# Token mixing of a gated MLP: the seventh feature chunk as seven block products on 64-column tiles of the matmul array

## Chip, cores, metric

One core of a Trainium2 chip. The metric is the device time of one execution in microseconds (us); medians are given with the lowest and highest run. Within 2% of the kernel before counts as "same".

Engines are named as in the profile: PE is TensorE's matmul, PEld its weight loads, DVE is VectorE, ACT is ScalarE, POOL is GpSimd, SP is SyncE, which here issues nearly all transfers. "Mixing" is the stage that multiplies by `w_sp`.

## The reference, cut to what matters

```python
x = A_x                                        # 1 x 2048 x 512, bf16
h = x + _A_ref(_layernorm(x), A_wqkv, A_wo)    # linear attention: num / den, times wo
h2 = h + _B_ref(_layernorm(h), B_w_in, B_w_sp, B_b_sp, B_w_out)

def _B_ref(x, w_in, w_sp, b_sp, w_out):        # w_in 512 x 1792, w_sp 2048 x 2048, w_out 896 x 512
    z = _gelu(x @ w_in)
    z1, z2 = z[..., :896], _layernorm(z[..., 896:])
    g = einsum('ts,bsf->btf', w_sp, z2) + b_sp[None, :, None]   # the token mixing
    return (z1 * g) @ w_out
```

The 896 features are seven chunks of 128.

## The kernel before: the parts that the change and the argument touch

Every operation is recorded with what it reads and writes. `ORDER` is a packed list that fixes the order of all operations on all engines, transfers included; it was searched in advance.

Six of the seven chunks are mixed in pairs (k, k + 3) by `cell`, with seven block products in place of eight (Strassen-Winograd). The combined operands t1, t2, t4 (of `w_sp`) and s1, s2, s4 (of z2) are made on VectorE. The seventh chunk is a plain product, twice 16 matmuls in each of two passes over pairs of token groups.

```python
def matmuls(out_ap, pairs, start=True, stop=True, onto=False, **k): ...   # one matmul for each (a, b) of pairs

def cell(k, lo, hi):                      # two chunks, two token groups: seven products of 8 matmuls
    ...
    matmuls(bank(A), [(z2[:, s, fl], wsp[:, s, lo]) for s in ss])
    act(bank(B), bank(A), ACT.Copy, GW)
    matmuls(bank(E), [(s1[:, s, :], t1[:, s, :]) for s in ss])
    ...

for p in range(NG // 2):
    lo, hi = (slice(tg * GW, (tg + 1) * GW) for tg in (p, p + NG // 2))
    last = KF - 1
    for tok, b in ((lo, EB[0]), (hi, EB[1])):           # the seventh chunk, plain
        matmuls(bank(b), [(z2[:, s, last * P:KF * P], wsp[:, s, tok]) for s in range(NT)])
        gate(last, tok, b, bsp[:, tok])
    ... combine(t1 ...), combine(t2 ...), combine(t4 ...)
    for k in range(HF):
        ... combine(s1 ...), combine(s2 ...), combine(s4 ...)
        cell(k, lo, hi)
```

Three further places play a part in what follows: the warm-up of PE at the start, the denominators of the attention, and the last sums with their stores.

```python
warmup(34, 103)                                          # 34 matmuls of 128 columns; 16 more a little later

for tg in range(NG):                                     # denominators of a token group
    PE(... zc x pqT on four tiles of 32 columns ...)
    act_exp(r_t, ..., ACT.Ln); act_exp(rcp, r_t, ACT.Exp, scale=-1.0)
    for c in range(KD): spread(first, c, ...)            # SP: four transfers r<-rcp, spread over the partitions
    dve(... tensor_tensor(pqT, pqT, r, ALU.mult) ...)    # needs those transfers
for n in range(NT):
    matmuls(bank(b), [(pqT[:, c, ...], m[:, c, :]) ...]) # "m,pqT" in the profile: needs that multiply

... tensor_tensor(h, psum, h) ...; store(n, slice(0, D), h[:, n, :])   # SP issues most of the stores
```

## Time and profile before

| | before |
|---|---|
| time, median (range) | 230.46 us (230.15 to 230.71, 3 runs) |
| span of the profiled execution | 228.4 us |
| from the start to the sum over pk | 44.48 us |
| from there to the first product with `win` | 19.68 us |
| from there to the last product with `win` | 43.05 us |
| mixing and output: from there to the start of the last matmul | 118.29 us |
| tail: from there to the end | 2.86 us |

The five stages are read from the start times of PE's groups in the timeline; they add up to the span. PE is the bound in all of them.

### The profile page before, as it was taken

The page shows a single profiled execution, that of the slowest core. Times are in us where ns is not written, and L with a number is a line of the kernel's source. Part 1 is how long each engine was busy: PE and PEld are TensorE (multiplying, and loading weights), DVE is VectorE, ACT ScalarE, POOL GpSimd, SP SyncE. Part 2 cuts the span into 40 slices and gives each one's busy share as a digit, 9 for nine tenths or more (in the row PEclk, how much of TensorE's full clock was granted, in tenths as well). Part 3 has the DMA queues.
Part 4 walks back from the last instruction along what each step waited for, and adds up shares of the span by engine and source line. Part 5 has one row for each costly group of instructions (what it writes and reads, how often), then busy time and mean ns, then how long its engine had stood idle before and what let it go on. Part 6 is the DMA issues. An engine that isn't in the chain of part 4 may idle for free.

```text
span 228.4 us, 3248 instructions
## 1 busy us (share of the span) xinstructions
PE 221.9 (97%) x1168; PEld 110.1 (48%) x1191; DVE 174.5 (76%) x349; ACT 108.5 (48%) x203; POOL 47.1 (21%) x134
## 2 busy tenths in 40 slices
PE   7999999999999999999999999999999999999995
PEld 7444444453344444544444444444455556555453
DVE  3899656638999786679998869864988985574395
ACT  5695753389989988999762010300021311122010
POOL 4444300000562694138820000000000000000000
PEclk9999999999999999999999999999999999999999
DMA  6736449927566244599904999200000002010004
GB/s 192 240 77 139 93 110 377 252 70 182 115 126 129 46 95 92 115 210 187 182 1 90 196 192 203 58 0 0 3 0 0 24 26 92 0 46 3 0 23 161
DMA packets 58896, 23.68 MB, mean 104 GB/s; under 512 B 48512, under 2 KB 58752, under 8 KB 58880
## 3 DMA queue, kind: packets, MB, share of 16 engines
q1 hardware_dynamic: 58176, 22.88, 44.2%
q10 hardware_dynamic: 704, 0.59, 0.9%
q8 instruction: 9, 0.15, 0.3%
q14 instruction: 7, 0.06, 0.1%
HBM read 7.47 MB, written 2.10 MB: 42 GB/s over the span
## 4 chain that ended last, share of the span: by engine, by line
PE 87%; DMA 4%; DVE 3%; ACT 3%; issue 1%; POOL 1%; SPq 1%; DVEq 0%
PE psum L402 69%; PE psum L659 6%; PE psum L813 6%; PE psum L816 4%; DMA x<-in_A_x_dram 2%; DMA hnT<-hn 1%; DVE st L510 1%; ACT ct L421 1%; SPq L432 1%; ACT pqT L421 0%; PE psum L724 0%; PE psum L680 0%; ACT z L421 0%; DVE h L988 0%; ACT sh L421 0%
## 5 line engine op out<-in xcount | busy, mean ns | idle before, releaser
L421 ACT ACTIVATE psum<-psum 128x256 f32<-128x256 f32 (+1 forms) x39 | 17.7, 468 | 86.7 <-PE psum L402 55.5
L402 PE MATMUL psum<-wsp,z 128*128 128x512 bf16 x201 | 47.8, 379 | 0.4
L402 PEld LDWEIGHTS psum<-wsp,z 128*128 128x128 bf16 x208 | 20.3, 98 | 23.0
L421 ACT ACTIVATE e<-psum 128x1024 bf16<-128x1024 f32 (+1 forms) x18 | 16.7, 927 | 14.1 <-PE psum L402 13.1
L402 PE MATMUL psum<-t,s 128*128 128x512 bf16 x95 | 22.3, 379 | 0.1
L402 PE MATMUL psum<-wsp 128*128 128x256 bf16 (+1 forms) x87 | 18.9, 313 | 0.2
L421 ACT ACTIVATE z1T<-psum 128x512 bf16<-128x512 f32 x28 | 15.7, 600 | 6.3 <-PE psum L402 5.7
L996 DVE TENSOR_TENSOR u<-psum,bsp 128x512 bf16<-128x512 f32 x16 | 11.0, 688 | 9.4 <-PE psum L402 9.2
L813 PE MATMUL psum<-win,hnT 128*128 128x512 bf16 x63 | 16.4, 379 | 0.3 <-DMA hnT<-hn 0.3
L402 PE MATMUL psum<-wout,z1T 128*128 128x256 bf16 (+1 forms) x81 | 16.2, 313 | 0.0
L659 PE MATMUL psum<-pk,xn 128*128 128x512 bf16 x64 | 15.3, 379 | 0.0
L402 PE MATMUL psum<-xnT,wqkv 128*128 128x512 bf16 x61 | 15.1, 379 | 0.2
L402 PE MATMUL psum<-m,pqT 128*128 128x512 bf16 x62 | 14.6, 380 | 0.4 <-DVE h L787 0.2
L402 PE MATMUL psum<-wqkv,xnT 128*128 128x512 bf16 x61 | 14.7, 379 | 0.2
L421 ACT ACTIVATE z<-psum 128x896 bf16<-128x896 f32 x16 | 14.4, 919 | 0.8 <-PE psum L816 0.5
L402 PEld LDWEIGHTS psum<-t,s 128*128 128x128 bf16 x96 | 9.4, 98 | 10.0
L581 DVE TENSOR_SCALAR e<-e 128x1024 bf16<-128x1024 bf16 (+1 forms) x18 | 7.0, 391 | 8.1 <-ACT e L421 7.9
L816 PE MATMUL psum<-win,hnT 128*128 128x384 bf16 x64 | 13.0, 326 | 0.0
L510 DVE BATCH_NORM_STATS2 st<-x 128x6 f32<-128x512 bf16 x15 | 9.9, 674 | 3.8 <-DMA x<-in_A_x_dram 3.8
L996 DVE TENSOR_TENSOR u<-psum,p 128x512 bf16<-128x512 f32 x12 | 8.3, 688 | 5.8 <-PE psum L402 5.8
L787 DVE SCALAR_TENSOR_TENSOR h<-psum,x 128x512 bf16<-128x512 f32 x16 | 10.7, 686 | 1.8 <-PE psum L402 1.7
L402 PEld LDWEIGHTS psum<-wsp 128*128 128x128 bf16 x90 | 8.7, 98 | 6.8 <-DVE wsp L1001 0.4
(126 smaller groups left out, 378.3 us busy)
## 6 DMA issues: line engine op xcount, KB each, us to landing
r<-rcp SPq DMA_DIRECT2D x16, 128.0 KB, 2.6
out_dram<-h SPq DMA_DIRECT2D x15, 128.0 KB, 1.7
win<-in_B_w_in_dram SPq DMA_DIRECT2D x2, 896.0 KB, 7.2
x<-in_A_x_dram SPq DMA_DIRECT2D x6, 256.0 KB, 4.3
wqkv<-in_A_wqkv_dram SPq DMA_DIRECT2D x2, 512.0 KB, 5.7
wout<-in_B_w_out_dram SPq DMA_DIRECT2D x1, 896.0 KB, 7.2
wo<-in_A_wo_dram SPq DMA_DIRECT2D x1, 512.0 KB, 5.9
bsp<-in_B_b_sp_dram SPq DMA_DIRECT2D x1, 512.0 KB, 4.4
```

The lines of the kernel that those rows point to most:

```text
L402: inst = pe.matmul(out_ap, lhsT=a, rhs=b, start=start and i == 0, stop=stop and i == len(pairs) - 1, **kw)
L421: return g.add("ACT", lambda ac: ac.activation(out_ap, in_ap, func, **kw), [in_ap, *extra], [out_ap] + ([accum] if accum is not None else []),
L432: return g.add(eng, lambda q: q.dma_start(out_ap, in_ap), [in_ap], [out_ap], cost=issue, lat=lat, dma=name, **k)
L510: dve(lambda v: v.bn_stats(s[:, 0:6], src[:, n, :]), [src[:, n, :]], [s[:, 0:6]], D)
L581: dve(lambda v: v.tensor_scalar(e, e, 1.0, EPS_PHI, op0=ALU.min, op1=ALU.add), [e], [e], w * GW, acc=4)
L659: inst = pe.matmul(bank(CB[c]), lhsT=xn[:, i, c * P:(c + 1) * P], rhs=pk[:, i, :], start=i == 0, stop=i == NT - 1)
L787: dve(lambda v, n=n, b=b, s=s: v.scalar_tensor_tensor(h[:, n, :], bank(b), 1.0, x[:, n, :], op0=ALU.mult, op1=ALU.add, accum_out=s[:, 0:1] ...
L813: pe.matmul(bank(b), lhsT=hnT[:, c, n * P:(n + 1) * P], rhs=win2[:, c, 0:GW], start=c == 0, stop=c == KD - 1)
L816: inst = pe.matmul(bank(b + 1, F2), lhsT=hnT[:, c, n * P:(n + 1) * P], rhs=win2[:, c, GW:FH], start=c == 0, stop=c == KD - 1)
L996: dve(lambda v: v.tensor_tensor(t, bank(b), add, ALU.add), [bank(b), add], [t], GW, ps=True)
```

## The change

The intent: seven block products for eight also for the seventh chunk. Split in halves of 64 features, its products have only 64 weight columns, half the array's width. So two of them run side by side on two column tiles, between the products of the other chunks. The arithmetic saves an eighth of 64 matmul steps.

```diff
-ORDER = "c-jTQ17HvU00h8Cwq47%ZQHhO...          (cut: the order of all operations, searched anew)
+ORDER = "c-jrs19Bh;00q&HBxBpQZQHhO...
+    def halves(pairs):                          # two products, matmul by matmul in turn
+        ...
+            for s in range(max(len(a) for _, a, _ in pairs)):
+                for o, a, start in pairs:
+                    if s < len(a):
+                        inst = pe.matmul(o, lhsT=a[s][0], rhs=a[s][1], start=start and s == 0, ...)
+    def last_cell(lo, hi):
+        ...
+        halves([(pb(Y, L), [(z2[:, s, fl], wsp[:, s, lo]) for s in ss], True),
+                (pb(Y, U), [(z2[:, HT + s, fh], t4[:, s, :]) for s in ss], True)])
+        act(pb(X, U), pb(Y, L), ACT.Copy, GW)
+        halves([...])                           # one product in two half sums, 4 pairs
+        halves([(pb(E, L), [(s1[:, s, :], t1[:, s, :]) for s in ss], True),
+                (pb(X, U), [(s2[:, s, :], t2[:, s, :]) for s in ss], False)])
+        act(pb(X, L), pb(X, U), ACT.Copy, GW)
+        halves([...])
+        ... four sums out of PSUM on VectorE, two gates
     for p in range(NG // 2):
-        last = KF - 1
-        for tok, b in ((lo, EB[0]), (hi, EB[1])):
-            matmuls(bank(b), [(z2[:, s, last * P:KF * P], wsp[:, s, tok]) for s in range(NT)])
-            gate(last, tok, b, bsp[:, tok])
...
         for k in range(HF):
+            if k == C6[p]:
+                ... four combinations of z2's blocks in the first pass
+                last_cell(lo, hi)
```

## The prediction

> **What bounds the kernel now.** I read the engine totals first, then the chain of work that ended last, then the stretches of the mixing stage, and last the TensorE timeline around the only place where the kernel already uses column tiles.
>
> ```profile
> span 228.4 us, 3248 instructions
> ...
> PE 221.9 (97%) x1168; PEld 110.1 (48%) x1191; DVE 174.5 (76%) x349; ACT 108.5 (48%) x203; POOL 47.1 (21%) x134
> ...
> PE 87%; DMA 4%; DVE 3%; ACT 3%; issue 1%; POOL 1%; SPq 1%; DVEq 0%
> ```
>
> TensorE is busy for 97% of the span and carries 87% of the chain. A busy PE need not be a dense one, so I compared counts with time in three stretches (end of the gated MLP's input products; first half of the token mixing; second half with the output products). The columns are the stretch, its length, then busy time and count of PE, PEld, DVE, ACT, POOL, then clock and DMA.
>
> ```profile
> 66.00:107.50 41.50, 41.29 (x204) 19.98 (x207) 33.20 (x79) 38.38 (x79) 22.18 (x59) 1.00 0.61 122
> 107.50:161.00 53.50, 53.24 (x246) 24.07 (x249) 43.23 (x71) 14.15 (x26) 7.21 (x17) 1.00 0.55 103
> 161.00:223.00 62.00, 61.68 (x344) 34.13 (x350) 46.26 (x93) 10.40 (x26) 0.00 (x0) 1.00 0.06 20
> ```
>
> In 107.5 to 161 us there are nearly only matmuls of 512 columns: 53.5 us over 246 records is 0.217 us each, at a granted clock of 1.00. Neighbouring matmuls of one product start 0.216 us apart, so PE starts one whenever the array can take it. The few steps of twice that length come about once in 50 matmuls, always 431 or 432 ns: lost records, not waits. From 66 us to the end PE never waits for anything by more than some tens of ns. So what the change is worth is what it takes from, or adds to, PE's own stream. VectorE has 53.5 - 43.2 = 10.3 us idle in the first stretch of mixing and 62.0 - 46.3 = 15.7 us in the second.
>
> Now the cost of a column tile. The sum over pk is sixteen matmuls, four side by side on tiles of 32 columns, between two normal products (start, length, what, count):
>
> ```profile
> 43.52 1.03 PE L659 MATMUL psum<-pk,xn 128*128 128x512 bf16 x4
> 44.48 1.05 PE L680 MATMUL psum<-pk,ones 128*32 128x512 bf16 x16
> 45.46 1.04 PE L659 MATMUL psum<-pk,xn 128*128 128x512 bf16 x4
> ...
> 44.48 0.55 PEld L680 LDWEIGHTS psum<-pk,ones 128*32 128x32 bf16 x16 [0.42 <-issue]
> 45.46 0.55 PEld L659 LDWEIGHTS psum<-pk,xn 128*128 128x128 bf16 x4 [0.42 <-issue]
> ```
>
> Two things are to be seen. Sixteen matmuls take 0.98 us from first to next (44.48 to 45.46): four steps of 0.216 us make 0.863, so four tiles do run at once, with different moving data. But there is a toll: the product before has four matmuls from 43.52, so the next start was due at 43.52 + 0.863 = 44.38 and came at 44.48 (+0.10); the way back was due at 44.48 + 0.863 = 45.34 and came at 45.46 (+0.12). The weight loader stands still for 0.42 us at both seams, where it otherwise loads ahead. The full-width product after the seam also starts its second matmul some 10 ns late. A round trip into column tiles and back thus costs about 0.22 us, as much as one matmul step. The denominators' four-matmul groups give the same: from the normal matmul at 50.21 to the second normal one after the group at 51.07 is 0.87 us where three steps would be 0.65.
>
> **What the Trainium skill says.** "TensorEngine Tiling (Array Packing)", section Tiling Modes: different tiles run independently, and "Mode switching requires drain". The trace agrees on both, with the 0.98 us for sixteen matmuls and the 0.22 us per round trip. Its section Restrictions says column tiling switches Fast Weight Load off; "TensorE: Matmul & The Clock Gate", section LDWEIGHTS, has a load last columns / 1.2 ns. The trace fits: 32 columns take 96 ns and 128 (fast) take 98. My estimate for 64 columns, from the 96 ns plus 32 / 1.2 of that page, is 123 ns; two at once on separate tiles still hide behind a 216 ns step, and each seam may cost some 0.02 us more than with 32. "VectorE: DVE Perf Modes", section on why a reduction can't run across partitions, calls each partition an independent lane: I take a 64-partition operation to last as long as a 128-partition one. No row of the kernel before shows that.
>
> **The change part by part.**
> *Removed:* the seventh chunk as a plain product, 2 token halves x 2 passes x 16 = 64 matmuls of 512 columns: 64 x 0.2158 = 13.81 us of PE.
> *Added on PE:* seven block products of 8 matmuls with 64 weight columns in each of 2 passes: 112 matmuls in 56 pairs (8 + 4 + 8 + 8 pairs a pass). If a pair takes one step, 56 x 0.2158 = 12.08 us. Gross gain 1.73 us, and no more: seven products for eight is worth an eighth of 13.8 us.
> *Added on PE, not in the intent:* seams. In the built instruction order the four paired groups of each pass stand apart, each between full-width products, since a copy or a sum has to come between them. That is 8 round trips x 0.22 = 1.76 us, or 8 x 0.24 = 1.9 us with the slower loads. This eats the whole gain: net +0.0 to +0.2 us.
> *Added on VectorE:* per pass four sums out of PSUM (like the 128x512 f32 sums at 0.688 us) = 2.75 us, twice 5.5 us; once four combinations of z2's blocks of 512 elements (like the 128x512 bf16 ones at 0.42 us) = 1.7 us. Together 7.2 us in 26 us of idle time, 4.4 of them in the first stretch's 10.3. The gates are as many as before.
> *Added on ScalarE:* four copies PSUM to PSUM at 0.584 us = 2.3 us, on an engine that is mostly idle there.
> *Moved:* the instruction order is a new one on all engines, from the first microseconds on. The plain chunk used to stand at the head of each pass, work for PE that needs no combination. Without it PE reaches combined operands earlier. From the end of the last z2 input product to the first product of t2 the new order has 76 steps = 16.4 us, and 92 steps = 19.9 us to the first paired group, which reads t4. Before, the last normalisation of z2 ended at 117.2, 9.8 us after that input product (107.4). In the new DVE order t2 then is finished after t1 (2.2), two sums s (1.2), one bias sum (0.6) and t2 (2.2) = 6.2, at 16.0 us; t4 after two more sums (1.2) and itself (2.2), at about 19.4 us. Both fit with 0.4 us to spare, so I put an expected wait of 0.2 us there.
>
> Sum: -13.81 + 12.08 + 1.8 + 0.2 = +0.3 us. 230.46 + 0.3 is about 230.8 us.
>
> **The rivals.**
> (a) Seams cost little, because the scheduler placed the groups where the loader has slack. Then the gain of 1.7 us shows: 228.7 us. Against it: four groups of the kernel before paid the 0.2 us each time, between quite different neighbours.
> (b) A pair of 64-column matmuls doesn't run side by side, or only in part (two weight loads of half width in a step, two PSUM banks). Then up to 56 more steps: +12.1 us, 242 us. Against it: four tiles ran at once with four different streams; what is untested is 64 columns, and tiles writing to different banks.
> (c) VectorE becomes the bound where the passes begin. Its chain of 2.2 us combinations is at the limit, as shown, and in 161 to 187 us it is already busy for 23.7 of 26.0 us. A bad placement there would cost 1 to 2 us: 232 us.
> (d) The new order changes the first 66 us, where PE loses about 3 us to waits in all (half of it round the denominators and the first transposed tiles). It can give or take half a microsecond for reasons that have nothing to do with the column tiles.
>
> **Range and chances.** The sum is +0.3; seams uncertain by 0.3 down and up, the new order by 0.7, waits for VectorE up to 1.5 upward. So 229.4 to 232.3 us. 2% is 4.6 us: faster by that is out of reach (gross gain 1.73), slower needs (b) or a bad (c), 4 in 100.
>
> **What would show it.** In the mixing stage the 112 narrow matmuls should come in pairs 3 to 4 ns apart with 0.216 us from pair to pair (wrong if 0.43). At each of the 8 groups the next start should come 0.09 to 0.13 us late going in and again coming out, with the weight loader idle for about 0.42 us (wrong if these are under 0.05). VectorE should go up by 7 us, to about 182, ScalarE by 2 us, and neither should end waits of PE by more than 0.5 us in all. Were the first 66 us to end earlier or later by over 0.7 us, the new order and not the chunk would have made the difference.

## The result, and the profile after

| | before | after |
|---|---|---|
| time, median (range) | 230.38 us (230.15 to 230.71, 6 runs) | 232.37 us (231.82 to 232.87, 6 runs) |
| ratio, 95% interval | | 1.0084, 1.0068 to 1.0101 |

A ratio here is the mean time of one kernel's fast runs over that of the other's in the same rounds, so it is not quite the ratio of the medians that stand beside it. The class is "same", as predicted. The predicted 230.8 us is 1.6 us too low, and 232.37 lies just outside the range. The changed kernel was run in two more batches as a control: 233.01 us (1.0128) and 233.77 us (1.0150). The distance to the kernel before thus differs between these batches, from 2.0 to 3.4 us, while the kernel before kept to 230.2 to 230.4. (The two later batches ran on two different chips; the record doesn't name that of the first. The third batch is compared with the runs of the kernel before from the batch ahead of it, on the same chip, and one more.)

The stages show three places where the time came from. All three columns of "after" are one and the same kernel:

| stage (us) | before | after | after, 2nd batch | after, 3rd batch |
|---|---|---|---|---|
| to the sum over pk | 44.48 | 44.73 | 44.95 | 44.60 |
| to the first `win` product | 19.68 | 20.00 | 20.13 | **21.51** |
| to the last `win` product | 43.05 | 43.05 | 43.05 | 43.05 |
| mixing and output | 118.29 | **118.97** | **118.97** | **118.96** |
| tail | 2.86 | **4.39** | **4.01** | **3.88** |
| span | 228.36 | 231.14 | 231.11 | 232.00 |

The page of the changed kernel: span, engine totals, the queue that brings PE its instructions (kind, packets, MB, share), and the chain.

```profile
span 231.1 us, 3391 instructions
...
PE 223.8 (97%) x1239; PEld 109.3 (47%) x1239; DVE 181.9 (79%) x361; ACT 110.7 (48%) x207; POOL 48.5 (21%) x134
...
q8 instruction: 10, 0.16, 0.3%
...
PE 85%; DVE 5%; ACT 3%; DMA 3%; issue 1%; POOL 1%; SPq 1%
```

The same queue's line on the page of the kernel before:

```profile
q8 instruction: 9, 0.15, 0.3%
```

VectorE went from 174.5 to 181.9 us and ScalarE from 108.5 to 110.7: the predicted 7 and 2 us. The eight sums on 64 partitions took 0.68 to 0.69 us each, as long as those on 128 (0.69), as the prediction had it. The line to note is q8: ten packets for nine.

**The mixing.** PE's timeline of the changed kernel round the first paired group (start, length, engine, line, operation, what, shape, count):

```profile
126.83 1.24 PE L407 MATMUL psum<-t,s 128*128 128x512 bf16 x5
128.00 0.40 PE L1036 MATMUL psum<-wsp,z 128*64 128x512 bf16 x1
128.01 0.40 PE L1036 MATMUL psum<-t,z 128*64 128x512 bf16 x1
128.24 0.38 PE L1036 MATMUL psum<-wsp,z 128*64 128x512 bf16 x1
...
129.54 0.38 PE L1036 MATMUL psum<-wsp,z 128*64 128x512 bf16 x1
129.54 0.38 PE L1036 MATMUL psum<-t,z 128*64 128x512 bf16 x1
129.85 1.90 PE L407 MATMUL psum<-wsp,s 128*128 128x512 bf16 x8
```

The two products of a pair start 3 to 4 ns apart in the trace, and pairs follow at 0.216 us (0.24 for the first). The five steps before the group end at 126.83 + 5 x 0.2158 = 127.91; the first pair comes at 128.00 (+0.09). The eighth pair ends its step at 129.76; the next full-width matmul comes at 129.85 (+0.10). With the slow first step this is 0.22 us for the round trip, as predicted.

A wait that was not predicted stands at 186 us, with the plain chunk no longer there to fill it (same view):

```profile
186.07 0.38 PE L407 MATMUL psum<-wout,z1T 128*128 128x512 bf16 x1
186.67 0.50 PE L407 MATMUL psum<-wout,z1T 128*128 128x256 bf16 x3 [0.22 <-DVE h L993]
```

The next start was due at 186.29 and came 0.38 us later: an output product waits for PSUM banks that VectorE has yet to empty. In the kernel before, no wait longer than some tens of ns stands in this stage. The predicted wait for t2 or t4 near 127 us did not come at all.

**The head.** SP's timeline, from the loads of the weights to the denominators, in the kernel before ("SPq" is the time in which SP issues transfers):

```profile
32.34 0.57 SPq L432 DMA_DIRECT2D win<-in_B_w_in_dram  x1
...
38.44 3.22 SPq L435 DMA_TRANSPOSE wsp<-in_B_w_sp_dram  x1
41.71 1.38 SPq L432 DMA_DIRECT2D wo<-in_A_wo_dram  x1
49.92 10.19 SPq L749 DMA_DIRECT2D r<-rcp  x12
```

The same view of the changed kernel in its third batch:

```profile
40.10 0.51 SPq L437 DMA_DIRECT2D win<-in_B_w_in_dram  x1
40.66 7.26 SPq L440 DMA_TRANSPOSE wsp<-in_B_w_sp_dram  x3
47.97 0.58 SPq L437 DMA_DIRECT2D win<-in_B_w_in_dram  x1
50.20 10.33 SPq L754 DMA_DIRECT2D r<-rcp  x12
```

In the new order three weight transposes hold SP for 7.26 us, and the second half of `win` is issued at 47.97 us instead of 32.34, just ahead of the transfers of r that the denominators wait for. What becomes of those transfers is told by the view of the tile r from 49 to 57 us; the kernel before:

```profile
DMA to landing us min/median/max: 2.6/2.6/2.7
```

And the changed kernel, third batch:

```profile
DMA to landing us min/median/max: 2.6/3.3/4.9
```

PE's timeline at the same place, kernel before:

```profile
53.74 0.40 PE L758 MATMUL psum<-pqT,zc 128*32 128x512 bf16 x4
54.08 1.90 PE L402 MATMUL psum<-xnT,wqkv 128*128 128x512 bf16 x7
55.81 3.62 PE L402 MATMUL psum<-m,pqT 128*128 128x512 bf16 x16
```

PE's timeline of the changed kernel, third batch (in brackets the idle time ahead of the group and what ended it):

```profile
53.74 1.90 PE L407 MATMUL psum<-xnT,wqkv 128*128 128x512 bf16 x7
55.57 0.40 PE L763 MATMUL psum<-pqT,zc 128*32 128x512 bf16 x4
57.56 3.63 PE L407 MATMUL psum<-m,pqT 128*128 128x512 bf16 x16 [1.59 <-DVE pqT L779]
```

VectorE's timeline of the same execution:

```profile
55.87 0.69 DVE L779 TENSOR_TENSOR pqT<-pqT,r 128x1024 bf16<-128x1024 bf16 x1 [1.41 <-DMA r<-rcp]
```

In the old order the eight matmuls with `wqkv` (one record is lost) stood between the denominators and the product with m, so an r that came up to 1.7 us late (8 x 0.216) would not have been felt. In the new order the product with m comes straight after. It needs the multiply by r, and PE waits as long as r is late. The Trainium skill, "DMA: Bandwidth & Descriptors", section "Issuing engines are not separate DMA queues", says that transfers run on the same 16 DMA engines and interleave. The trace agrees that more was in flight: from 50 to 53.5 us the engines moved 116 GB/s before and 286 in this run. But the traffic by itself does not make r late: in `a_short`, a run described below, they moved 293 GB/s and r landed in 2.6 to 2.9 us.

In the run on record r was hardly late. The view of the tile r from 49 to 57 us says:

```profile
DMA to landing us min/median/max: 2.5/2.7/3.2
```

PE stood idle for 0.09 us at the first product with m. Its other waits in this stage, in its timeline:

```profile
60.08 1.90 PE L407 MATMUL psum<-m,pqT 128*128 128x512 bf16 x8 [0.27 <-DVE pqT L779]
62.55 1.04 PE L407 MATMUL psum<-m,pqT 128*128 128x512 bf16 x4 [0.58 <-DVE h L792]
```

And in the kernel before:

```profile
59.65 3.91 PE L402 MATMUL psum<-m,pqT 128*128 128x512 bf16 x16 [0.22 <-DVE h L787]
64.16 1.04 PE L813 MATMUL psum<-win,hnT 128*128 128x512 bf16 x4 [0.27 <-DMA hnT<-hn]
```

So the new order has a cost of its own, besides the late r. PE's work in the stage up to the first `win` product is the same in both orders. In the three profiles of the new order in which r landed within 3.2 us, this stage takes 20.00 us. In the twelve profiles of the old order it takes 19.35 to 19.39 seven times, 19.65 to 19.71 four times, with a wait for hnT, and once 20.77, with a long one. A later r comes on top of the 20.00: 0.13 to 2.22 us in the other five profiles of the new order.

**The tail.** The longest issue of a store on SP near the end, by its timeline, in the kernel before:

```profile
225.83 0.44 SPq L432 DMA_DIRECT2D out_dram<-h  x1
```

And in the changed kernel:

```profile
225.22 2.40 SPq L437 DMA_DIRECT2D out_dram<-h  x1
```

Three more stores stand behind the second one. The last store was issued by 226.27 us before and by 229.09 after, although VectorE's last sum ended 0.73 us after the start of the last matmul in both. The tenth packet of q8, 16 KB of instructions for PE, began at 225.34 us and took 1.90 us. The Trainium skill, "Runtime: NRT & Kernel Launch", section "Instruction fetch mechanics", says that instructions come in 16 KiB blocks of 256 and that the cost of crossing a boundary is "mostly hidden". The size agrees (0.16 MB in ten packets), and so does the number: the ten packets start 254 PE instructions apart on the mean. PE did not stall at it either, but the store beside it did. The change adds 48 matmuls and 48 weight loads. I count PE's stream as twice its weight loads (matmul records can be lost, loads were not) plus semaphore and drain instructions: 2406 before, 2508 after.

### The profile page after: what moved, and what is told of

The parts are those of the page before. It is cut to its first block, busy times and chain, and to the rows that moved or that the text cites. A ratio compares the mean times of both kernels' runs of the same rounds, so it can differ in the third digit from the quotient of the medians.

```text
span 231.1 us, 3391 instructions
## 1 busy us (share of the span) xinstructions
PE 223.8 (97%) x1239; PEld 109.3 (47%) x1239; DVE 181.9 (79%) x361; ACT 110.7 (48%) x207; POOL 48.5 (21%) x134
## 4 chain that ended last, share of the span: by engine, by line
PE 85%; DVE 5%; ACT 3%; DMA 3%; issue 1%; POOL 1%; SPq 1%
PE psum L407 61%; PE psum L664 6%; PE psum L818 6%; PE psum L1036 6%; PE psum L821 5%; DMA x<-in_A_x_dram 3%; DVE h L993 2%; DVE st L515 1%; ACT r L426 1%; DVE h L964 1%; ACT e L426 1%; SPq L437 1%; POOL st L539 1%; ACT rcp L426 0%; PE psum L729 0%
## 5 line engine op out<-in xcount | busy, mean ns | idle before, releaser
L426 ACT ACTIVATE psum<-psum 128x256 f32<-128x256 f32 (+2 forms) x43 | 20.1, 477 | 84.8 <-PE psum L407 57.1
L407 PE MATMUL psum<-wsp,z 128*128 128x512 bf16 x144 | 33.9, 379 | 0.0
L407 PEld LDWEIGHTS psum<-wsp,z 128*128 128x128 bf16 x144 | 13.9, 98 | 16.3 <-issue 0.8
L407 PE MATMUL psum<-wsp 128*128 128x256 bf16 (+1 forms) x90 | 19.9, 315 | 0.0
L407 PE MATMUL psum<-wout,z1T 128*128 128x256 bf16 (+1 forms) x83 | 16.8, 315 | 0.2 <-DVE h L993 0.2
L1001 DVE TENSOR_TENSOR u<-psum,p 128x512 bf16<-128x512 f32 x14 | 9.6, 688 | 6.6 <-PE psum L407 6.5
L539 POOL TENSOR_SCALAR st<-st 128x1 f32<-128x1 f32 x10 | 3.8, 379 | 39.0 <-ACT sh L426 35.5
L1002 DVE TENSOR_TENSOR z1T<-u,z1T 128x512 bf16<-128x512 bf16 x28 | 11.5, 421 | 0.4
```

Of the source, the lines that this page charges most:

```text
L407: inst = pe.matmul(out_ap, lhsT=a, rhs=b, start=start and i == 0, stop=stop and i == len(pairs) - 1, **kw)
L426: return g.add("ACT", lambda ac: ac.activation(out_ap, in_ap, func, **kw), [in_ap, *extra], [out_ap] + ([accum] if accum is not None else []),
L539: pool(lambda p: p.tensor_scalar(s[:, 2:3], s[:, 0:1], s[:, 0:1], -1.0 / (n * n), op0=ALU.mult, op1=ALU.mult), [s[:, 0:1]], [s[:, 2:3]], 240)
L1001: dve(lambda v: v.tensor_tensor(t, bank(b), add, ALU.add), [bank(b), add], [t], GW, ps=True)
L1002: dve(lambda v: v.tensor_tensor(z, t, z, ALU.mult), [t, z], [z], GW, acc=2)
```

## The experiments

Eighteen runs in five batches, each beside runs of the kernel before on the same chip: sixteen new kernels, and the changed kernel twice more as a control. Each was executed six times in the fast state (`b_pairs16` four times, `after_third` five). In brackets stand the ratio to the kernel before and its 95% interval. All results were correct.

**What a round trip costs: `b_pairs4`, `b_pairs16`.** The kernel before, with 8 of the 16 steps of each of the four plain products made as two matmuls of 64 columns, in one run of 8 or in 4 runs of 2. The two differ only in the number of round trips, 4 or 16. (Both have the short warm-up of `a_short`.)

```diff
+    PAIRED = (4, 5, 6, 7, 8, 9, 10, 11)          # b_pairs16: (1, 2, 5, 6, 9, 10, 13, 14)
+                if s in PAIRED:
+                    for r in (slice(0, H), slice(H, P)):
+                        inst = pe.matmul(psum[r, b, :], lhsT=w[:, r], rhs=m, **kw)
```

> The kernel before (warm-up in wide matmuls, so that the longer stream brings no tenth refill) with 8 of the 16 steps of each of the four plain products of the seventh chunk made as pairs of 64-column tiles, in one run of 8 steps: same arithmetic, same number of steps, 4 round trips into column tiles. Seam theory (0.22 us each): +0.9 us, about 231.3 us. Rival (a pair of 64-column tiles is slower than a full step): 32 pair steps, so up to +6.9 us if they do not overlap. Rival (seams are free): 230.4 us.

> As b_pairs4, with the same 32 pair steps, but in four runs of 2 steps in each product: 16 round trips instead of 4. Seam theory: 12 more round trips at 0.22 us make +2.6 us over b_pairs4, about 233.9 us. Rival (the cost is per pair, not per change of mode): the same time as b_pairs4.

Measured: 230.93 us (1.0045, 1.0024 to 1.0065) and 233.64 us (1.0158, 1.0136 to 1.0181). The mixing took 119.20 and 121.92 us. (121.92 - 119.20) / 12 = 0.227 us a round trip from the traces, (233.64 - 230.93) / 12 = 0.226 from the times. With four round trips the stage is +0.91 us over the kernel before, 4 x 0.227. PE's timeline of `b_pairs16`:

```profile
123.81 0.38 PE L1039 MATMUL psum<-wsp,z 128*128 128x512 bf16 x1
124.12 0.62 PE L1037 MATMUL psum<-wsp,z 128*64 128x512 bf16 x4
124.68 0.61 PE L1039 MATMUL psum<-wsp,z 128*128 128x512 bf16 x2
```

From 123.81 the next start was due at 124.03 and came at 124.12 (+0.09). Two pairs take 0.43 us, to 124.55; the next came at 124.68 (+0.13, with some 0.02 for the slow first pair). So the round trip is a fixed cost, whatever its length, and eight cost 1.81 us.

**Fewer PE instructions: `a_short`.** The changed kernel with the warm-up in fewer, wider matmuls.

```diff
-    warmup(34, 103)      # 128 columns each; the second warm-up: 16
+    warmup(9, 427)       # 512 columns each; the second warm-up: 4
```

> The changed kernel with the same warm-up time on TensorE, made of 13 wide matmuls instead of 50 narrow ones: 74 instructions fewer in TensorE's stream, everything else as it was. In the profile of the changed kernel a tenth 16 KB instruction packet starts at 225.34 us, when 2485 of TensorE's 2508 recorded instructions have started, and the store issued at 225.22 us takes 2.40 us instead of 0.33 to 0.45; three more stores queue behind it. Theory A (the extra instructions bring a tenth refill into the last stores): with 74 fewer there are nine refills, no long store issue, and the end comes 1.2 to 1.6 us earlier: about 231.0 us. Theory B (the new order of stores and last sums is the cause, the packet is a coincidence): still a long tail, 232.2 to 232.5 us. Both: a granted clock of 1.0 and seams as before.

Measured: 231.22 us (1.0053, 1.0036 to 1.0070), nine refills, the longest store issue 0.46 us, tail 2.84 us. In the trace the tail went as theory A has it. The 1.15 us against the first run of the changed kernel are from different batches, and since the head varies between batches they cannot all be given to the tail. Nor is a faster time with the short warm-up a proof of the tail: see `a_head` below, where the same edit gains 0.9 us without a refill at the end.

**More PE instructions: `b_long`, `b_cols`.** The kernel before with 48 matmuls of 8 columns more in the warm-up; and with 13 of the 16 matmuls of each plain product cut into two of 256 columns.

```diff
+            for _ in range(EXTRA.pop(0)):                      # b_long
+                inst = pe.matmul(bank(7, 8), lhsT=warm, rhs=warm[:, 0:8], start=True, stop=True)
```
```diff
+                n = GW // 2 if s < 13 else GW                  # b_cols
+                for c in range(0, GW, n):
+                    inst = pe.matmul(bank(b, n, c), lhsT=w[s], rhs=m[s][:, c:c + n], ...)
```

> The kernel before with 48 tiny matmuls (8 columns) added to the warm-up, while TensorE waits for x anyway: 96 instructions more in TensorE's stream, as the change has. Theory A: a tenth 16 KB packet some 20 to 30 instructions before the end, among the last stores, and up to 1.5 us more: 230.9 to 231.9 us. Theory B: nothing happens, 230.4 us (230.2 to 230.7). If the packet comes but falls between two store issues, it costs less than 0.5 us and says only that the collision is a matter of luck.

> The kernel before with 13 of the 16 matmuls of each of the four plain products cut into two of 256 columns: 52 matmuls and 52 weight loads more, which brings TensorE's stream to the length of the changed kernel's (2504 instructions against 2506), without column tiles, and without the delay at the head that spoilt b_long. The cuts themselves cost 52 x 2.5 ns = 0.13 us. Theory A (refill in the last stores): a tenth 16 KB packet some 20 instructions before the end, a store issue of over 1 us beside it, and 231.0 to 231.9 us. Theory B (order of the stores): 230.3 to 230.6 us and no long issue.

`b_long`: 231.22 us (1.0047, 1.0014 to 1.0079), but of no use for the question. The extra matmuls delayed the head by 1.5 us (the sum over pk came at 46.02), and its 2502 instructions brought no tenth refill. `b_cols`: 231.34 us (1.0050, 1.0024 to 1.0076), mixing 118.42 (+0.13, as expected for the cuts), 2510 instructions, a tenth refill at 225.53 us, one store issue of 1.04 us, tail 3.40. Its profiled run also waited 1.5 us for a transposed tile in the head, so its time does not settle the size of the tail.

**Six round trips for eight, another order: `a_merge`, `a_merge_head`.** `a_short` with the four-pair group put next to the eight-pair group that follows it and the order searched anew from 100 us; the second one also has the old order of the head.

```diff
-ORDER = "c-jrs19Bh;00q&HB...
+ORDER = ...              # a_merge: new from 100 us; a_merge_head: before's order for the first 90 us as well
```

> a_short with another instruction order from the mixing stage on: the 4-pair group stands right before the following 8-pair group in both passes, so 6 round trips into column tiles instead of 8. The first 100 us keep the changed kernel's order. Seam theory: 2 x 0.226 = 0.45 us less than a_short, about 230.75 us. Rival (seams hidden by other waits): as a_short, 231.2 us.

> As a_merge, but the first 90 us in the order of the kernel before. If the new order of the first part cost time (in the two profiles the stretch from the sum over pk to the last z2 product is 62.73 us before and 63.05 us after), this is 0.3 us less than a_merge, about 230.4 us. If that was chance of one profile, it is the same as a_merge.

Measured: 232.00 us (1.0087, 1.0065 to 1.0110) and 231.33 us (1.0065, 1.0031 to 1.0101). A miss: the mixing stayed at 118.96 and 118.97 us. In the mixing of `a_merge` new waits (0.11 us at 124.7, 0.19 at 164.9, 0.06 at 212) ate most of the 0.45 us that two round trips are worth; in `a_merge_head` one of 0.40 at 114 did. Both also lost time before the mixing, in the stage to the last `win` product: 43.73 us (with a wait of 0.62 at 104.4) and 43.36, against 43.05. My model of the order had no VectorE jitter in it. For the head this pair gives a hint only: of the 0.67 us between the two, the profiles have 0.64 in the head (20.00 us against 19.36 to the first `win` product), but also 0.37 in the next stage, and the two intervals overlap.

**Two round trips for eight: `a_bridge`.** The changed kernel with four of the full-width products that stood between paired groups made as column pairs themselves. PE then goes into column tiles once a pass. The order is new, with the old head.

```diff
+    SPLIT = {(0, 0): (5, 6), (1, 1): (6,), (1, 2): (0,)}
-        matmuls(bank(A), [(z2[:, s, fl], wsp[:, s, lo]) for s in ss])
+        (pairs if 0 in narrow else matmuls)(bank(A), [(z2[:, s, fl], wsp[:, s, lo]) for s in ss])
```
(the same for two more products of `cell`; `pairs` issues each matmul as two of 64 columns)

> The changed kernel with four full-width products, those that fill the time of the copies between the paired groups, made as pairs of 64-column tiles too, at the same number of steps; so TensorE stays in column tiles from a pass's first paired group to its last: 2 round trips instead of 8. Head in the order of the kernel before. Narrow warm-up kept: with 60 more instructions (2566) the tenth refill should fall some 80 instructions before the end, ahead of the last stores. Seam theory: 1.73 us gained, 0.45 us paid, 0.5 us waits at 183 to 186 us kept: 229.4 to 229.9 us, below the kernel before. Rival (a narrow pair costs more than a step): above 230.4 us.

Measured: 229.91 us (0.9985, 0.9955 to 1.0016), mixing 117.81 us: 1.16 less than the changed kernel, where 6 x 0.226 = 1.36 was to be saved. The time can't be told from that of the kernel before; its profile lost 0.47 us ahead of the mixing (43.52 us to the last `win` product). Its stream of 2572 instructions has the tenth refill at 219.4 us, ahead of the last stores, and a tail of 2.85. So more instructions can do less harm; it depends on where a refill falls.

**The control, more instructions on purpose, and two more orders: `after_again`, `a_pad`, `a_bridge2`, `a_bridge3`.** `a_pad` is the changed kernel with the first product of the cells of the first pass cut into halves of 256 columns. `a_bridge2` has the edits of `a_bridge` with the changed kernel's order up to 122 us, `a_bridge3` with the old order to 88 us and a search that also asked for slack.

```diff
-        matmuls(bank(A), [(z2[:, s, fl], wsp[:, s, lo]) for s in ss])           # a_pad
+        (cut if p == 0 and k < 4 else matmuls)(bank(A), [(z2[:, s, fl], wsp[:, s, lo]) for s in ss])
```

> Control: the changed kernel as it is, once more, beside the three below on the same chip. Expected 1.0084 of the kernel before (231.5 to 232.4 us), a tenth refill of the PE stream near 225 us in its profile, and at least one of the last stores issued in over 1 us. If it came out below 1.006, what I found of its tail would be a matter of chance from one execution to the next, and not of where the refill falls.

> The changed kernel with MORE for PE to do: the first product of four cells of the first pair of token groups is cut into halves of 256 columns, 32 matmuls and 32 weight loads more (+64 PE instructions), in its first half of the mixing. The refill that collided with the stores must then come some 32 x 0.216 = 6.9 us earlier, near 218.4 us, before the first stores (221 us). Theory (the tail is a refill of the PE stream that falls on the last stores): the tail is back to 2.8 to 2.9 us, the cut halves cost about +0.1 us as in the run with cut columns, and the kernel is 1.0 to 1.4 us FASTER than the changed kernel of this batch (0.9945 to 0.9965 of it, 1.003 to 1.005 of the kernel before). Rival 1 (the number of instructions as such, or of refills, costs): not faster, +0.1 to +0.3 us. Rival 2 (the slow stores belong to the kernel's own late order, not to the refill): unchanged within 0.3 us, with slow stores in the profile.

> The four full-width filler products as column pairs (2 round trips instead of 8), but with the changed kernel's own order of the head and of everything to 122 us, the rest searched anew. Theory of the seams: 6 round trips fewer x 0.226 = 1.36 us less in the mixing than the changed kernel, less what the 32 more pairs cost and the wait at 185 us gone: mixing 117.5 to 117.9 us from the first output-side product to the last matmul, against 118.97. Theory of the head order: the head costs +20.00 us from the sum over pk to the first win product as in the changed kernel, so this is 0.2 to 0.4 us slower than a_bridge3. Time 0.998 to 1.001 of the kernel before. Rival (seams not the cause): mixing 118.6 to 119.0, time 1.003 or more.

> As a_bridge2, with the kernel before's order of the head (to 88 us) and an order searched from there for slack as well as for length. Theory: mixing 117.4 to 117.8 us, the head +19.35 to +19.7 as in the kernel before, no refill on the stores: 229.3 to 229.8 us, 0.995 to 0.998 of the kernel before, so faster than both kernels. Rival (the search of the order buys nothing that the chip keeps, as with the merged order): 0.9985 or more.

`after_again`: 233.01 us (1.0128, 1.0100 to 1.0156), slower than its first batch; tenth refill at 225.7, one store issued in 2.03 us, as expected. `a_pad`: 231.88 us (1.0078, 1.0054 to 1.0102), so with more work it was 1.13 us faster than the control. The edit was mis-sized: there are three such cells in a pass and not four, so 48 instructions were added instead of 64, and the refill came at 223.3 us and not at 218.4. That was still early enough: longest store issue 0.45 us, tail 2.84. (One store was issued beside that refill, in 0.33 us, so not every overlap makes a store slow; a much earlier one, at 201.6 us beside another refill, took 1.91 us without harm.) Its profiled run, though, was the slowest of its six and had a wait of 1.69 us in the head.

`a_bridge2`: 230.91 us (1.0035, 1.0010 to 1.0060), mixing 117.75. `a_bridge3`: 229.49 us (0.9979, 0.9962 to 0.9995), mixing 117.89, a little above the expected 117.4 to 117.8. These two have the same products and two round trips; 1.42 us lie between them. Their profiles are 1.64 us apart, of which 1.13 is in the head (20.78 against 19.65) and 0.67 before the sum over pk. That is far more than the 0.2 to 0.4 that I expected. `a_bridge3` is the only version that beats both kernels: by 0.7 us in the medians, by 0.5 us (0.1 to 0.9) in the ratio.

**The parts undone one by one: `before_short`, `a_head`, `a_head_short`.** The kernel before with the short warm-up; the changed kernel with the old order for everything before 92 us; and that with the short warm-up.

```diff
-ORDER = "c-jrs19Bh;00q&HB...        # a_head, a_head_short: mixing in the changed kernel's order,
+ORDER = "c-jTQ0{|NU00XdMw{6...      # head in the order of the kernel before
-    warmup(34, 103)                 # before_short, a_head_short
+    warmup(9, 427)
```

> The kernel before with the warm-up as 9 + 4 matmuls of 512 columns in place of 34 + 16 of 128: 74 PE instructions fewer, nothing else. Theory: the kernel before has no refill on its stores, so there is nothing to gain: 0.998 to 1.002 of the kernel before, and the 1.15 us that the same edit won on the changed kernel came from the tail. Rival (the warm-up itself is worth time, by the clock or by an earlier head): 0.994 to 0.997.

> The changed kernel with one thing undone: the order of everything that starts before 92 us is that of the kernel before; the mixing keeps the changed kernel's order, with its 8 round trips, and the warm-up is the narrow one. Theory: the head is +19.35 to +19.7 us from the sum over pk to the first win product in the profile (20.0 to 20.1 in the changed kernel), mixing 118.9 to 119.0, and the tenth refill still falls on the stores near 225 us (tail 3.9 to 4.5): 1.005 to 1.009 of the kernel before, that is 0.4 to 0.9 us faster than the changed kernel. Rival (the head order costs nothing, the differences seen are chance): 1.009 to 1.012.

> Both other causes taken away: the head's order of the kernel before, and the short warm-up, so that nine refills are enough. What is left is the mixing as changed, with its 8 round trips. Theory: tail 2.8 to 2.9, head +19.35 to +19.7, mixing 118.9 to 119.0, which is +0.68 us over the kernel before: 1.0025 to 1.004 (230.8 to 231.1 us). Rival 1 (a further cause that I have not found): 1.005 or more. Rival 2 (the head costs nothing): as the first run with the short warm-up, 1.005.

`before_short`: 230.26 us (1.0013, 0.9985 to 1.0040): the short warm-up by itself is worth nothing. `a_head_short`: 230.86 us (1.0028, 1.0006 to 1.0049), head 19.35, mixing 118.97, tail 2.86. With the head and the tail of the old kernel, what is left is +0.28%, or 0.64 us, and the mixing alone accounts for 0.68. No further cause is needed.

`a_head`: 231.75 us (1.0064, 1.0041 to 1.0088), head 19.71. The expected tenth refill was not there. The old head order needs three wait instructions fewer on PE: 2505 instead of 2508, and nine refills, tail 2.85. So its profile has no cost but the mixing (and 0.18 us lost at 123.6), and yet its time is 0.9 us above that of `a_head_short`. The two profiled executions are 0.39 us apart, which the head (0.36) and the 0.18 us cover; what makes up the rest I cannot say. It matters for the argument: the short warm-up is worth 0.9 us here although neither profile has a refill on the stores, so what it won on the changed kernel is no measure of the tail.

**Whether three instructions decide: `a_trim`, `a_head_more`, `after_third`.** Two warm-up matmuls off the changed kernel (2504), two more on `a_head` (2509), and the control (2508).

```diff
-    warmup(34, 103)
+    warmup(32, 103)      # a_trim; a_head_more: 36
```

> The changed kernel with two narrow warm-up matmuls fewer (34 to 32), so 2504 PE instructions instead of 2508, and nothing else. Theory (the tenth refill comes above some number between 2505 and 2508): nine refills, no store issued in over 0.6 us, tail 2.8 to 2.9, and 0.8 to 1.4 us faster than the control of this batch. Rival (the refill comes at a time or a phase, not at a number; or the short warm-up won by something else): ten refills, a slow store, and the time of the control within 0.4 us.

> The kernel with the changed mixing and the old head order (2505 PE instructions, nine refills) with two narrow warm-up matmuls more: 2509. Theory: the tenth refill comes back, near 224.5 us, on the last stores: one of them issued in 0.9 us or more, tail 3.4 to 4.5, 232.1 to 232.9 us (1.008 to 1.011 of the kernel before) where the same kernel with 2505 had 231.75 (1.0064). Rival: nine refills, tail 2.85, 1.005 to 1.0075.

> Control: the changed kernel, as it is, on the chip of the two above: 1.0084 to 1.0128 of the kernel before, as in its two batches so far, with ten refills and a slow store.

The refills came as the theory of the number has it, both ways. The longest issue of a store in `a_trim`, by SP's timeline:

```profile
227.87 0.45 SPq L437 DMA_DIRECT2D out_dram<-h  x1
```

And in `a_head_more`:

```profile
225.22 1.37 SPq L437 DMA_DIRECT2D out_dram<-h  x1
```

`a_trim` had nine and a tail of 2.86, `a_head_more` ten and a tail of 3.69. The times did not follow: `a_trim` 233.62 us (1.0135, 1.0095 to 1.0175) against 233.77 (1.0150, 1.0130 to 1.0170) of the control; `a_head_more` 231.78 us (1.0071, 1.0047 to 1.0095) against 231.75 of `a_head`. In the profile, what `a_trim` won at the tail (1.02 us) it lost for the greater part in the head, by waiting 2.49 us for r where the control waited 1.77. The largest and clearest difference of this batch is again the head: 1.99 us between `after_third` and `a_head_more`, with 21.51 against 19.39 in the profile.

**All twenty profiles together.** Eight profiles have the new order of the head. `win` was issued in them at 46.28 to 48.98 us, and PE's first product with m came late in every one (counted from the start that was due, which is 0.18 us more than the idle time in brackets): 0.27 us where `win` came at 46.28, 46.43 and 47.12, 0.40 at 47.81, 1.77 at 47.97, 1.69 and 1.05 at 48.23, 2.49 at 48.98. Twelve have the old order, with `win` at 31.9 to 34.7 us, and none of them waits there for r. The slowest landing of r goes with the issue of `win`, counted from the sum over pk: 2.8 to 2.9 us for an issue 1.8 to 1.9 us after it, 3.2 for 2.4, 3.6 for 2.9, 4.2 to 4.9 for 3.4 to 3.5, and 5.7 for 3.8.

Five have a refill at 225 to 227 us: a slowest store issue of 1.04 to 2.40 us and tails of 3.40 to 4.39. In the other fifteen no store issue in the last 15 us took over 0.56 us, and the tails are 2.84 to 2.89. The head shows the same effect: in five profiles a refill starts within 0.1 us of the issue of `wo`, which then takes 1.37 to 1.43 us in place of 0.58. It is not a rule, though. In `a_head` a refill starts just as near and the issue takes 0.58, and in `a_pad`, `a_bridge2` and `a_bridge3` a refill near the end ran beside store issues of 0.33 to 0.56 us.

## Why the prediction was wrong, point by point

- **"So many steps for so many"**: right. Pairs run side by side, with 0.216 us from pair to pair; rival (b) is dead.
- **Seams**: right, 8 x 0.22 predicted and 8 x 0.226 measured by itself. The cost that the intent left out eats the 1.73 us. The load times were misjudged without harm: the prediction says that the trace fits the page on weight loads, but only the equality does (96 ns for 32 columns, 98 for a fast 128), not the length (see the last section).
- **The wait of 0.2 us for t4 at 127 us**: zero; t4 was ready at 126.58 us, 1.4 us ahead of the paired group, where the prediction left 0.4. In its place came 0.38 us at 186 us for PSUM banks, with another 0.08 just before, and 0.09 at 109 us. The whole stage is +0.68 us where the sum had +0.3, well within what the range allowed.
- **The sum has no term for the end**: by its profile, this is the step that failed first. I counted 48 matmuls more only as steps of PE's time, not as instructions that have to be fetched. The stream went from 2406 to 2508 instructions; somewhere above 2505 a tenth refill comes, and here it falls on the last stores: +1.53 us in the profile of the run on record, +1.0 to +1.5 in the three profiles of this kernel. That the number decides is shown in both directions, by four instructions fewer and four more. That it costs as much in an execution's time is not: `a_pad` against its control says 1.13 us, the other two pairs (`a_trim` against its control, `a_head_more` against `a_head`) under 0.2. It stays open how much of the time without a profile belongs to it.
- **"The new order by 0.7"**, with rival (d)'s "half a microsecond": the second step that failed. I looked at where the new order sent the matmuls and the VectorE operations of the mixing, and gave the head an allowance either way, without reading its transfers. The size was inside the allowance in the run on record: +0.57 us up to the first `win` product (44.73 + 20.00 against 44.48 + 19.68), so the sign of being wrong, 0.7 us, did not show there; in the third batch it did, with +1.95. What was wrong is the kind of cost. It is not chance in either direction but a loss: 20.00 us where the old order mostly has 19.35, and a late r on top. (The 0.25 us before the sum over pk is within the spread of that stage: 44.08 to 45.50 in the old order, 44.45 to 45.16 in the new.) That the order of the head costs time is shown by two pairs with the same mixing stage to within 0.15 us: `after_third` against `a_head_more` (1.99 us) and `a_bridge2` against `a_bridge3` (1.42). That the `win` load is what makes r late is read from the traces: from the landings and the waits, which grow with the time of its issue. No kernel moved that load alone, and three weight transposes moved together with it, so these remain a rival.
- **The range**: its terms do not give it. Around 230.8 us they make 229.8 to 233.3 when added up, or 230.0 to 232.5 as the root of the sum of squares; 229.4 to 232.3 is neither.

Summed, in the profile: +0.57 in the head, +0.68 in the mixing, +1.53 in the tail are 2.78 us, and the profiled execution was 232.87 - 230.09 = 2.78 us longer. That execution was the slowest of its six, though; the medians are 1.99 us apart. From the times alone, the parts put back one by one give another sum: +0.64 us for the mixing (`a_head_short`), 0.8 to 0.9 more with the narrow warm-up (`a_head`), and 0.5 to 2.0 more with the new head (the three batches of the changed kernel, partly on other chips). The part that comes with the narrow warm-up is the one whose cause is not shown.

The hint was there before the change: beside a refill at 41.68 us, the issue of `wo` took 1.38 us where other such issues took 0.58. I did not see it then.

The intended gain of 1.73 us is there in the count of steps, since pairs follow at one step each, and the seams ate it. With two round trips for eight and the old head, `a_bridge3` keeps 0.40 us of it in the mixing (117.89 against 118.29).

## What to carry to other kernels

When a change comes with a new order of instructions, compare the order of the transfers too, in the stages it was not meant for: what was moved beside a transfer that someone waits for, and what no longer covers its landing. Count the switches between tile shapes as matmul steps of their own, and merge narrow products into one run even at the price of making full-width ones narrow. Count instructions as well as time: a handful can add an instruction fetch at a bad place, so look where the fetches of the busiest engine fall against the last stores.

## What the Trainium skill lacked or had wrong

- "TensorEngine Tiling (Array Packing)", section Key Properties: it says that a mode switch drains PE, but not what this costs. Here it is 0.226 us for the way into 128x64 tiles and back (0.09 in, 0.10 out, 0.02 for the slower first pair, 0.01 for the second full-width matmul after it), whether 2 or 8 pairs stand between.
- "TensorE: Matmul & The Clock Gate", section LDWEIGHTS: it states columns / 1.2, from which I estimate 27 ns for 32 columns and 53 ns for 64, while 96 ns and 108 to 109 ns were recorded here in column tiles. My estimate of 123 ns for 64, from the measured 96 and the page's slope, was too high as well. Two such loads hide behind a step of 0.216 us.
- "Runtime: NRT & Kernel Launch", section "Instruction fetch mechanics": "mostly hidden" held for PE, but in five of five profiles with a refill at 225 to 227 us one store issue took 1.04 to 2.40 us instead of 0.33 to 0.45. The page's blocks of 256 instructions agree with the 254 between packets, but it does not say where in a stream the last fetch falls: here 2505 instructions make nine refills and 2508 ten.
- "DMA: Bandwidth & Descriptors", section "Issuing engines are not separate DMA queues": it has the interleaving, not what it costs a small transfer. The spread of r landed 2.5 to 3.1 us after its issue in the old order and up to 5.7 us after it (`a_trim`) where a weight load was issued shortly before, but in 2.6 to 2.9 us in `a_short`, with as many bytes in flight.
